# Order of VectorE's exponential tiles, forced emptying, booked durations and buffers by layer kind in a four-layer attention kernel

## The chip, the cores and the metric

The kernel runs on one core of one Trainium2 chip. The metric is the device time of one execution in microseconds. Five engines matter here: TensorE (PE in the profile, PEld its weight loads), VectorE (DVE), ScalarE (ACT), GpSimd (POOL) and SyncE (SP), which issues the DMAs. Each engine works through its own instructions in the order in which they were built; between engines, semaphores make one wait for another.

## The reference

Four layers, A, B, A, B, over one sequence of 2048 positions with 512 features. Each layer adds to x an attention over the layer-normed x, with 32 heads of 16 features:

```python
qkv = (x @ wqkv).reshape(B, S, 3, H, Dh).transpose(2, 0, 3, 1, 4)
q, k, v = qkv[0], qkv[1], qkv[2]
scores = einsum("bhqd,bhkd->bhqk", q, k) * Dh ** -0.5
# layer A only: scores = where(0 <= i - j < 256, scores, -1e9)
p = softmax(scores, axis=-1)
o = einsum("bhqk,bhkd->bhqd", p, v).transpose(0, 2, 1, 3).reshape(B, S, D) @ wo
x = x + A(layernorm(x)); x = x + B(layernorm(x)); x = x + A(layernorm(x)); x = x + B(layernorm(x))
```

A is the sliding window, 256 keys wide (layers 0 and 2, "window layers"); B looks at all 2048 keys (layers 1 and 3, "full layers").

## The kernel before

**Tiles.** Scores are made transposed, with keys on the partitions. The 32 heads are taken as eight groups of four, and the queries as four chunks of 512; one group with one chunk is called a quad, so a layer has 32 quads. A quad of a full layer goes over 16 blocks of 128 keys. For each block TensorE makes two PSUM tiles `s` of 128 x 2 x 512 (two heads each, L754), ScalarE takes their exponential into two tiles `e` (L762), and TensorE multiplies these with the values into the accumulator `acc` (L827). A quad of a window layer has three steps of two tiles (scores L758, exponential L762); GpSimd zeroes what lies outside the window (L919, L922), and TensorE multiplies with the values (L929). There are two PSUM buffers for `s` and `EB` = 5 buffers for `e`.

**The queue of value products.** `pvq` holds the value products that are not yet given to TensorE. In a window layer `flush(2)` keeps two steps in it after the scores of a new one; in a full layer `flush(1)` keeps one.

**VectorE's exponential tiles.** In a full layer, key block `DJ` = 7 of a quad can have its exponentials made on VectorE instead of ScalarE. `expect` announces a quad's unit, which may take up to two tiles `d`. `unit` lets TensorE make the scores into a separate PSUM tile `b` (L772), VectorE turn them into a fixed-point exponent (L778, 128 x 1024), and then appends six steps to VectorE's queue number 3: for each half of the tile, step a (L786, L787: integer operations), step b (L793, L794) and step c (L797, L798: a polynomial). `units` decides whether there is still time for another tile before the quad's end, by the planner's own clock. If a quad has fewer than two tiles by its last two blocks, its block 7 is made last, with ScalarE making what is missing (the "own" case in `attn_full`; the exponential then has a bias, `lead`). Otherwise the unit's value product is given as soon as it is ready, or by force with the quad's last block (`unit_values`).

**The planner.** The order of the instructions of a full layer is written out by the Python code while it builds. It keeps two clocks: `clock` for TensorE, moved by `spent`, and `vt_` for VectorE, moved by `vec`. VectorE's work waits in five queues `VQ`: 0 for splitting projected queries and keys, 1 for finishing a quad's output, 2 for the layer norm, 3 for the exponential tiles, 4 for checks of the weights (`verify`). `soon` appends a step with a booked duration. `drain()` without a number gives steps while VectorE's clock is less than `AHEAD` past TensorE's, the first queue first; queue 3 goes behind queue 4 when the foremost unit is not that of the quad in work:

```python
order = VQ[:2] + VQ[3:4] if PH["mid"] else VQ if not UX or UX[0]["quad"] == PH["quad"] else VQ[:3] + VQ[4:] + VQ[3:4]
```

`drain(4)` gives all that stands in queues 0 to 3 at once. It is called ahead of the value product of block 7, in the own case and in the forced case. After a quad's last value product, `epilogue` empties queues 0 and 1 and then copies `acc` out of PSUM to `sa` (L432, L433, inside `join`); the next quad's first value product overwrites `acc` and so waits for that copy.

**Side work.** The projections, the output product, the layer norms and the weight checks of this and the next layer are cut into `Work` pieces, which `Side` hands to TensorE between the attention's own products. `CW` is the chain of weight checks, 32 parts of one load and five VectorE instructions (L370 to L376); each part waits for the one before it.

Of the kernel before, what the change touches and what calls it, by code (L numbers as in the profile page):

```python
# [10 lines left out]
F32 = mybir.dt.float32  # L11
# [9 lines left out]
P = 128  # L21
# [14 lines left out]
EB, XB, XNB, WB, VB, OB = 5, 4, 4, 2, 3, 5  # L36
# [159 lines left out]
def fast_path(ctx, tc, flag, a_x, a_wqkv, a_wo, b_wqkv, b_wo, out):  # L196
# [11 lines left out]

    ps_x = ExitStack()
# [10 lines left out]
    OL, OFREE = [], set()  # L220
# [28 lines left out]
    def drain(upto=None):  # L249

        if upto is not None:
            if PH["mid"] and upto > 2:
                give(VQ[3])
            for q in VQ[:upto]:
                while q:
                    while q[0][2] and not q[0][2]():
                        PH["side"].one(True)
                    give(q)
            return
        while vt_[0] <= clock[0] + AHEAD:  # L260
            order = VQ[:2] + VQ[3:4] if PH["mid"] else VQ if not UX or UX[0]["quad"] == PH["quad"] else VQ[:3] + VQ[4:] + VQ[3:4]
            q = next((q for q in order if q and (q[0][2] is None or q[0][2]())), None)
            if q is None:
                return
            give(q)
# [124 lines left out]
    def phase(l):  # L390

        PH["full"], PH["win"] = l is not None and l % 2 == 1, l is not None and l % 2 == 0
# [352 lines left out]
    def exps(name, kt, qt, pr, pieces, **bias):  # L745
# [15 lines left out]
        e = pp.tile([P, 2, QC], F32, name=f"e{name}", tag="e", bufs=EB)  # L761
# [3 lines left out]
    def unit(u):  # L765
# [10 lines left out]
        t = pp.tile([P, 2, QC], I32, name=f"d{n}", tag="d", bufs=2)  # L776
        vec(1.2)
# [3 lines left out]
        for h in range(2):  # L781
# [20 lines left out]
            for us, f in ((0.92, a), (1.2, b), (1.2, c)):  # L802
                soon(3, us, f)

    def units():
# [4 lines left out]
        if u["quad"] == PH["quad"]:  # L810
            queued = sum(us for q in VQ[:4] for us, _, _ in q)
            if max(vt_[0], clock[0]) + queued + 8.5 > PH["end"]:
                return False
# [4 lines left out]
    def expect(l, c, qd, kts, qt, us):  # L818

        UX.append(dict(n=f"{l}_{c}_{qd}", quad=(l, c, qd), kt=kts[DJ // 8], qt=qt, e=[], left=0, at=0.0, shut=False, ready=clock[0] + us))  # L820
# [9 lines left out]
    def unit_values(l, c, qd, force=False):  # L830
# [4 lines left out]
        if force:  # L835
            drain(4)
# [35 lines left out]
    def attn_full(l, c, qd, kt, qt, a):  # L872
        js = [j for j in range(NT) if j != DJ]
        own = [None]
        for j in js + [DJ]:
# [17 lines left out]
            def pv(j=j, es_=es_):  # L893
                if j == js[-1] and not own[0] and UX and UX[0]["quad"] == (l, c, qd):
                    unit_values(l, c, qd, True)
                if j == DJ:
                    drain(4)
# [208 lines left out]
    def attention(l, works):  # L1106
# [5 lines left out]
        for t in range(NHT if l == 3 else 1):  # L1112
            for c in range(NQ):
# [12 lines left out]
                for qd in qds:  # L1126
# [6 lines left out]
                    a = acc[qd % 2 if win else 0]  # L1133
                    PH["side"], PH["quad"], PH["end"] = sd, (l, c, qd), clock[0] + 1.81 * NT
# [163 lines left out]
    def side1():  # L1298
        m = [(ty, s) for ty in range(2) for s in range(4)]
        a = [CW(*x, [("C", *y)] if y else [("Q", 1, 2)]) for y, x in zip([None] + m, m)]  # L1300
# [73 lines left out]
```

## Time and profile before

| | us |
|---|---|
| median of three runs | 2881.78 (2879.71 to 2884.62) |
| the profiled execution | 2883.96 |
| its span, first to last instruction | 2882.2 |
| busy TensorE, ScalarE, VectorE, GpSimd | 2526.1, 2292.2, 2021.3, 479.3 |
| stretch of layer 0 (window) | 55 to 446 |
| stretch of layer 1 (full) | 504 to 1482 |
| stretch of layer 2 (window) | 1500 to 1808 |
| stretch of layer 3 (full) | 1864 to 2848 |

The stretches reach from a layer's first exponential to its last. Between them TensorE ends the projections of the next layer. The mean granted TensorE clock was 0.975.

How to read it: a group line gives source line, engine, operation, out<-in, shapes and count, then busy us and the mean ns of one, then the idle time of the engine before them and what ended most of it. A wait line reads "engine tile line <- whom it waited for: us in total, times, longest us". A row of the timeline has the start and the length in us, engine, line and operation, how many follow each other (x), and in brackets the idle time before it. All line numbers are those of the kernel before.

### The profile page before, as it was taken

How to read it: one execution, taken by the hardware profiler on the slowest of the kernel's cores; microseconds unless marked ns; L12 is line 12 of the kernel's file. 1: busy time of each engine (PE TensorE's matmuls, PEld its weight loads, DVE VectorE, ACT ScalarE, POOL GpSimd, SP SyncE). 2: the span in 40 equal slices, each digit the busy share in tenths (PEclk: the TensorE clock that was granted, in tenths of full speed). 3: DMA queues.
4: the chain of work that ended last, by engine and by line, in shares of the span. 5: the costliest groups of instructions: out<-in, count | busy, mean ns of one | idle time of the engine just before them, and what ended most of it. 6: DMA issues, size and time to landing. Idle time of an engine off the chain costs nothing.

```text
span 2882.2 us, 112925 instructions
## 1 busy us (share of the span) xinstructions
PE 2526.1 (88%) x50177; PEld 1098.3 (38%) x50177; DVE 2021.3 (70%) x3882; ACT 2292.2 (80%) x2576; POOL 479.3 (17%) x1047
## 2 busy tenths in 40 slices
PE   7779989999998998889888887898899889888886
PEld 3233334443433443344333332543344434333332
DVE  5564454587787767768877555477788777888886
ACT  4565653999998997889865666399899989888995
POOL 1445551000000000000014667000000000000000
PEclk9999999999999999999999999999999999999998
DMA  8887866222223223222336554523223333333433
GB/s 278 227 229 232 238 177 200 65 80 80 85 91 94 86 86 97 85 76 83 114 103 195 173 149 132 161 67 102 75 89 93 99 91 102 94 98 114 123 116 112
DMA packets 335042, 359.71 MB, mean 125 GB/s; under 512 B 113616, under 2 KB 250320, under 8 KB 328144
## 3 DMA queue, kind: packets, MB, share of 16 engines
q1 hardware_dynamic: 334544, 352.40, 40.3%
q8 instruction: 394, 6.46, 0.9%
q14 instruction: 104, 0.85, 0.1%
HBM read 239.60 MB, written 96.99 MB: 117 GB/s over the span
## 4 chain that ended last, share of the span: by engine, by line
ACT 34%; PE 31%; DVE 21%; issue 8%; DMA 4%; POOL 1%; SPq 1%; ACTq 0%; DVEq 0%; POOLq 0%
ACT e L762 33%; PE b L419 9%; PE acc L827 8%; PE acc L929 4%; PE s L754 3%; PE b L416 2%; DVE d L778 2%; PE s L758 2%; PE bs L419 2%; DVE x L701 2%; DVE dp L797 2%; DVE dp L794 1%; DVE dp L793 1%; DVE d L798 1%; DVE d L787 1%
## 5 line engine op out<-in xcount | busy, mean ns | idle before, releaser
L762 ACT ACTIVATE e<-s 128x1024 f32<-128x1024 f32 (+2 forms) x2304 | 2150.2, 1043 | 315.7 <-PE s L754 150.5
L827 PE MATMUL acc<-e,vt 64*17 64x512 f32 x15496 | 1069.1, 596 | 26.8 <-DVE sa L432 26.8
L754 PE MATMUL s<-qt,kt 64*32 64x512 f16 x15496 | 827.9, 382 | 112.4 <-ACT e L762 88.8
L754 PEld LDWEIGHTS <-kt 64*32 64x32 f16 x15496 | 374.7, 90 | 837.6 <-issue 764.4
L827 PEld LDWEIGHTS acc<-e,vt 64*17 64x17 f32 x15496 | 271.8, 93 | 117.5 <-DVE sa L432 28.3
L922 POOL TENSOR_SCALAR_AFFINE_SELECT e<-e 128x256 f32<-128x256 f32 x512 | 228.9, 450 | 211.4 <-ACT e L762 209.6
L919 POOL TENSOR_SCALAR_AFFINE_SELECT e<-e 128x256 f32<-128x256 f32 x448 | 191.5, 432 | 138.7 <-ACT e L762 137.8
L758 PE MATMUL s<-qt,kt 64*128 64x384 f16 (+2 forms) x1408 | 130.8, 280 | 90.5 <-ACT e L762 72.7
L929 PE MATMUL acc<-e,vt 128*17 128x384 f32 (+2 forms) x2816 | 199.5, 395 | 4.3 <-POOL e L919 3.4
L540 POOL TENSOR_TENSOR sq_h<-sp_h 128x512 bf16<-128x512 f16 x27 | 39.7, 1471 | 912.2 <-DVE sp_h L534 892.2
L778 DVE TENSOR_SCALAR d<-b 128x1024 int32<-128x1024 f32 x111 | 135.4, 1220 | 77.9 <-PE b L772 77.9
L540 POOL TENSOR_TENSOR sq<-sp 128x512 bf16<-128x512 f16 x28 | 41.0, 1464 | 891.9 <-DVE sp L534 836.1
L419 PE MATMUL b<-xc,w 128*128 128x512 f16 x696 | 163.3, 385 | 7.4 <-DMA w<-wd 5.0
L797 DVE SCALAR_TENSOR_TENSOR dp<-dp,dm 128x512 f32<-128x512 f32 x222 | 158.4, 714 | 6.6
L794 DVE SCALAR_TENSOR_TENSOR dp<-dp,dm 128x512 f32<-128x512 f32 x222 | 154.5, 696 | 7.7
L798 DVE SCALAR_TENSOR_TENSOR d<-dp,d 128x512 f32<-128x512 f32 x222 | 153.6, 692 | 7.5
L793 DVE SCALAR_TENSOR_TENSOR dp<-dm 128x512 f32<-128x512 f32 x222 | 154.4, 695 | 0.2
L432 DVE TENSOR_SCALAR sa<-acc 128x512 f32<-128x512 f32 x64 | 44.2, 690 | 132.1 <-PE acc L827 131.9
L720 DVE STREAM_TRANSPOSE ot<-acc 128x512 f32<-128x512 f32 x64 | 45.6, 712 | 119.3 <-PE acc L929 119.1
L758 PEld LDWEIGHTS <-kt 64*128 64x128 f16 x1408 | 54.3, 95 | 195.2 <-issue 168.7
L419 PEld LDWEIGHTS <-w 128*128 128x128 f16 x816 | 76.8, 99 | 121.9 <-issue 35.5
L416 PE MATMUL b<-xc,w 64*32 64x512 f16 x2688 | 115.0, 379 | 5.3 <-DVE j L433 3.9
(151 smaller groups left out, 2606.6 us busy)
## 6 DMA issues: line engine op xcount, KB each, us to landing
kt<-kf SPq DMA_DIRECT2D x128, 512.0 KB
qt<-qs SPq DMA_DIRECT2D x128, 256.0 KB
xd<-x SPq DMA_DIRECT2D x96, 256.0 KB
x<-xd SPq DMA_DIRECT2D x96, 256.0 KB
w<-wd SPq DMA_DIRECT2D x22, 1024.0 KB
kt<-kw SPq DMA_DIRECT2D x64, 256.0 KB
qs<-sp SPq DMA_DIRECT2D x48, 256.0 KB
wo<-wd SPq DMA_DIRECT2D x12, 1024.0 KB
```

The lines of the kernel that those rows point to most:

```text
L419: nc.tensor.matmul(ps, a, b, start=(i == 0), stop=(i == len(pairs) - 1))
L754: nc.tensor.matmul(ps[g:g + 32, h], kt[R * h:R * h + R, pr, kc + g:kc + g + 32], qt[R * h:R * h + R, pr], start=True, stop=True, skip_grou ...
L758: nc.tensor.matmul(ps[:, h, s0:s0 + wd_], kt[R * h:R * h + R, pr, kc:kc + P], qt[R * h:R * h + R, pr, qc:qc + wd_], start=True, stop=True)
L762: nc.scalar.activation(e[:, :, w0:w1], ps[:, :, w0:w1], AF.Exp, scale=SCALE, **bias)
L778: nc.vector.tensor_scalar(t, ps, SCALE * LOG2E * 2.0 ** 23, -2.0 ** 30, op0=ALU.mult, op1=ALU.max)
L793: nc.vector.scalar_tensor_tensor(p[0], f, POLY[3], f, op0=ALU.add, op1=ALU.mult)
L794: nc.vector.scalar_tensor_tensor(p[0], p[0], POLY[2], f, op0=ALU.add, op1=ALU.mult)
L797: nc.vector.scalar_tensor_tensor(p[0], p[0], POLY[1], m[0].bitcast(F32), op0=ALU.add, op1=ALU.mult)
L827: nc.tensor.matmul(acc[r][32 * h:32 * h + DH + 1, :], V[l, qd // 4, j // 8][k, j % 8, 4 * (qd % 4) + h, :], es[h // 2][k, h % 2, :], start ...
L919: nc.gpsimd.affine_select(v, v, pattern=[[0, 2], [-1, P]], compare_op=ALU.is_gt, fill=0.0, base=0, channel_multiplier=1)
L922: nc.gpsimd.affine_select(v, v, pattern=[[0, 2], [1, P]], compare_op=ALU.is_ge, fill=0.0, base=0, channel_multiplier=-1)
L929: nc.tensor.matmul(a[32 * h:32 * h + DH + 1, q * P:(q + nb) * P], V[l, (4 * c + j) // 4][:, j % 4, 4 * qd + h, :], es_[h // 2][:, h % 2, s ...
```

## The change

- `EB` becomes a pair: seven buffers of `e` in window layers and five in full layers. The buffers lie in a pool of their own, closed and opened anew in `phase` when the kind of layer changes; the two buffers of `d` move into this pool.
- Units get a running number, and quads of full layers are counted in `PH["i"]`. Queue 3 keeps its place ahead of queue 4 as long as the foremost unit belongs to the quad in work or to one before it.
- `complete(u)` replaces `drain(4)` in both places: it gives steps of queue 3 until the unit that is needed has none left. The other queues, and tiles of later units, stay where they are.
- Booked durations: the fixed-point step 1.3 instead of 1.2; steps a, b, c 0.82, 1.45, 1.45 instead of 0.92, 1.2, 1.2; the time that must be left before the quad's end for a further tile 9.0 instead of 8.5.
- The chain of weight checks may start after the upper values of layer 1's first chunk (`("V", 1, 0, (1,), 0)`) instead of after the queries of its third (`("Q", 1, 2)`).

The diff:

```diff
--- before.py
+++ after.py
@@ -33,7 +33,7 @@
 LOG2E = 1.4426950408889634
 MM = 0.222
 HEAD_START = 100
-EB, XB, XNB, WB, VB, OB = 5, 4, 4, 2, 3, 5
+EB, XB, XNB, WB, VB, OB = (7, 5), 4, 4, 2, 3, 5
 RINGS = WB, VB
 L_MIN = 2.0 ** -90
 L_SUM = 2.0 ** 60
@@ -206,6 +206,8 @@
     ps_c = pool("ps_c", 1, space=bass.MemoryType.PSUM)
     ps_s = pool("ps_s", 2, space=bass.MemoryType.PSUM)
 
+    pe_x = ExitStack()
+    ctx.push(pe_x)
     ps_x = ExitStack()
     ctx.push(ps_x)
     dp = pool("scr", 1, space=bass.MemoryType.DRAM)
@@ -217,7 +219,7 @@
     XC, XN, V, O, OT, KM, PH = {}, {}, {}, {}, {}, {}, {"free": 0.0, "busy": False, "mid": False}
     WT, ST, pend = {}, {}, []
     VQ, vt_, UX = [deque() for _ in range(5)], [0.0], deque()
-    OL, OFREE = [], set()
+    OL, OFREE, QN = [], set(), [0]
 
     clock, DONE, XNR, ONR = [0.0], {}, {}, {}
 
@@ -258,7 +260,7 @@
                     give(q)
             return
         while vt_[0] <= clock[0] + AHEAD:
-            order = VQ[:2] + VQ[3:4] if PH["mid"] else VQ if not UX or UX[0]["quad"] == PH["quad"] else VQ[:3] + VQ[4:] + VQ[3:4]
+            order = VQ[:2] + VQ[3:4] if PH["mid"] else VQ if not UX or UX[0]["i"] <= PH["i"] else VQ[:3] + VQ[4:] + VQ[3:4]
             q = next((q for q in order if q and (q[0][2] is None or q[0][2]())), None)
             if q is None:
                 return
@@ -389,6 +391,10 @@
 
     def phase(l):
 
+        if l is not None and PH.get("es") != l % 2:
+            PH["es"] = l % 2
+            pe_x.close()
+            PH["ep"] = pe_x.enter_context(tc.tile_pool(name=f"exps{l}", bufs=EB[l % 2]))
         PH["full"], PH["win"] = l is not None and l % 2 == 1, l is not None and l % 2 == 0
         if PH["full"] or not PH["win"] and "pool" not in PH or l is None and PH.get("halves"):
             ps_x.close()
@@ -758,7 +764,7 @@
                 nc.tensor.matmul(ps[:, h, s0:s0 + wd_], kt[R * h:R * h + R, pr, kc:kc + P],
                                  qt[R * h:R * h + R, pr, qc:qc + wd_], start=True, stop=True)
         spent(0.23 if PH["full"] else 0.27)
-        e = pp.tile([P, 2, QC], F32, name=f"e{name}", tag="e", bufs=EB)
+        e = PH["ep"].tile([P, 2, QC], F32, name=f"e{name}", tag="e")
         nc.scalar.activation(e[:, :, w0:w1], ps[:, :, w0:w1], AF.Exp, scale=SCALE, **bias)
         return e
 
@@ -773,8 +779,8 @@
                                  u["qt"][R * h:R * h + R, pr], start=True, stop=True, skip_group_check=True)
         spent(0.27)
         PH["free"] = clock[0] + 1.5
-        t = pp.tile([P, 2, QC], I32, name=f"d{n}", tag="d", bufs=2)
-        vec(1.2)
+        t = PH["ep"].tile([P, 2, QC], I32, name=f"d{n}", tag="d", bufs=2)
+        vec(1.3)
         nc.vector.tensor_scalar(t, ps, SCALE * LOG2E * 2.0 ** 23, -2.0 ** 30, op0=ALU.mult, op1=ALU.max)
         u["e"].append(t.bitcast(F32))
         u["left"] += 2
@@ -799,7 +805,7 @@
                 u["left"] -= 1
                 PH["mid"] = False
                 u["at"] = vt_[0] + 0.4
-            for us, f in ((0.92, a), (1.2, b), (1.2, c)):
+            for us, f in ((0.82, a), (1.45, b), (1.45, c)):
                 soon(3, us, f)
 
     def units():
@@ -809,7 +815,7 @@
             return False
         if u["quad"] == PH["quad"]:
             queued = sum(us for q in VQ[:4] for us, _, _ in q)
-            if max(vt_[0], clock[0]) + queued + 8.5 > PH["end"]:
+            if max(vt_[0], clock[0]) + queued + 9.0 > PH["end"]:
                 return False
         if not PH["busy"] and clock[0] >= PH["free"]:
             unit(u)
@@ -817,7 +823,13 @@
 
     def expect(l, c, qd, kts, qt, us):
 
-        UX.append(dict(n=f"{l}_{c}_{qd}", quad=(l, c, qd), kt=kts[DJ // 8], qt=qt, e=[], left=0, at=0.0, shut=False, ready=clock[0] + us))
+        QN[0] += 1
+        UX.append(dict(n=f"{l}_{c}_{qd}", quad=(l, c, qd), kt=kts[DJ // 8], qt=qt, e=[], left=0, at=0.0, i=QN[0], shut=False, ready=clock[0] + us))
+
+    def complete(u):
+
+        while u["left"]:
+            give(VQ[3])
 
     def values_of(l, qd, j, es, first, last):
 
@@ -833,7 +845,7 @@
         if u["quad"] != (l, c, qd) or u["shut"]:
             return False
         if force:
-            drain(4)
+            complete(u)
         elif len(u["e"]) < 2 or u["left"] or clock[0] < u["at"]:
             return False
         UX.popleft()
@@ -894,7 +906,7 @@
                 if j == js[-1] and not own[0] and UX and UX[0]["quad"] == (l, c, qd):
                     unit_values(l, c, qd, True)
                 if j == DJ:
-                    drain(4)
+                    complete(own[0])
                 values_of(l, qd, j, es_, j == 0, j == (DJ if own[0] else js[-1]))
             yield pv
 
@@ -1131,6 +1143,7 @@
                     if nxt and not win:
                         expect(l, c, qd + 1, *nxt, 6.0)
                     a = acc[qd % 2 if win else 0]
+                    PH["i"] = PH.get("i", 0) + (not win)
                     PH["side"], PH["quad"], PH["end"] = sd, (l, c, qd), clock[0] + 1.81 * NT
                     began, u = clock[0], 0
                     for f in (attn_win if win else attn_full)(l, c, qd, *ops, a):
@@ -1297,7 +1310,7 @@
 
     def side1():
         m = [(ty, s) for ty in range(2) for s in range(4)]
-        a = [CW(*x, [("C", *y)] if y else [("Q", 1, 2)]) for y, x in zip([None] + m, m)]
+        a = [CW(*x, [("C", *y)] if y else [("V", 1, 0, (1,), 0)]) for y, x in zip([None] + m, m)]
         a += [Q(1, c, False) for c in (2, 3)]
         for c in range(3):
             a += [OO(1, c), T(2, c)] + ([Q(2, c - 1, False)] if c else []) + [K(2, c, False)] + ([VV(2, c, False)] if c < 2 else [])
```

## Prediction

> **What bounds the kernel now.** I read the head of the page first, then the busy time by stage, then the waits of each kind of stage, then two short timelines.
>
> ```profile
> span 2882.2 us, 112925 instructions
> PE 2526.1 (88%) x50177; PEld 1098.3 (38%) x50177; DVE 2021.3 (70%) x3882; ACT 2292.2 (80%) x2576; POOL 479.3 (17%) x1047
> 55.00:446.00 391.00, 339.71 (x2952) 135.38 (x2951) 203.66 (x476) 237.96 (x308) 196.19 (x486) 0.94 0.78 222
> 504.00:1482.00 978.00, 886.13 (x21944) 390.50 (x21936) 741.63 (x1363) 903.74 (x973) 37.32 (x28) 0.98 0.28 86
> 1500.00:1808.00 308.00, 253.03 (x2553) 100.39 (x2552) 184.13 (x459) 195.65 (x228) 195.75 (x479) 1.00 0.53 157
> 1864.00:2848.00 984.00, 877.82 (x21438) 384.12 (x21438) 784.00 (x1339) 900.31 (x966) 39.72 (x27) 0.99 0.31 97
> ```
>
> The last four rows are layers 0 (window), 1 (full), 2 (window) and 3 (full): length, then busy PE, PEld, DVE, ACT, POOL, granted clock, DMA share, GB/s. In a full layer ScalarE sets the pace: 903.7 us of 978, about 0.931 us for each of its 971 exponential tiles. What is lost there is 74 and 84 us of idle ScalarE. In a window layer TensorE is nearest to full, and lacks 51 us (391.0 - 339.7) in layer 0 and 55 us (308.0 - 253.0) in layer 2.
>
> The waits of layer 0, of layer 2 (between them a line of dots), then of layers 1 and 3:
>
> ```profile
> PE s L758 <- ACT e L762: 24.9, 32, 1.6
> ACT e L762 <- PE acc L929: 21.7, 36, 5.1
> ...
> PE s L758 <- ACT e L762: 47.8, 59, 1.0
> ACT e L762 <- PE acc L929: 24.8, 49, 1.0
> ACT e L762 <- POOL e L919: 13.9, 22, 0.6
> ...
> ACT e L762 <- PE s L754: 70.4, 42, 15.8
> ...
> ACT e L762 <- PE s L754: 80.2, 59, 7.1
> ```
>
> So in the window layers scores wait for ScalarE, and ScalarE for buffers; in the full layers ScalarE waits for scores, in few and long pieces.
>
> **The change, part by part.**
>
> *Seven buffers of e in the window layers.* A stretch of layer 2 without side work:
>
> ```profile
> 1791.01 0.39 PE L758 MATMUL s<-qt,kt 64*128 64x128 f16 x4
> 1791.19 1.94 ACT L762 ACTIVATE e<-s 128x1024 f32<-128x1024 f32 x2 [0.64 <-PE acc L929]
> 1792.01 1.39 POOL L922 TENSOR_SCALAR_AFFINE_SELECT e<-e 128x256 f32<-128x256 f32 x2
> 1792.27 0.40 PE L758 MATMUL s<-qt,kt 64*128 64x128 f16 x4 [0.87 <-ACT e L762]
> 1792.59 1.06 PE L929 MATMUL acc<-e,vt 128*17 128x256 f32 x16
> 1793.36 0.40 POOL L919 TENSOR_SCALAR_AFFINE_SELECT e<-e 128x256 f32<-128x256 f32 x1
> 1793.58 0.39 PE L758 MATMUL s<-qt,kt 64*128 64x256 f16 x4
> 1784.00:1804.00 20.00, 13.39 (x190) 5.27 (x191) 17.95 (x41) 14.99 (x16) 19.06 (x43) 1.00 0.74 183
> ```
>
> One step (two tiles) takes 1793.58 - 1791.01 = 2.57 us. The queue of value products is two steps deep: four tiles are held while two are made, six in all. With five buffers the sixth exponential starts only when a value product has ended (0.64 us idle), and the next scores need its PSUM bank (0.87 us idle on PE). With seven no tile waits so. Then a step is paced by the slowest of three: PE's own 2.57 - 0.87 = 1.70 us; ScalarE's two tiles at 1.94 - 1.02 = 0.92 us each, about 1.9 us with the handing over; or GpSimd, whose 960 selects over 192 steps are five a step. In the last row, columns as before, 43 selects take 19.06 us of 20: 2.2 us a step. So of each wait 0.20 us stays if ScalarE paces, 0.50 us if GpSimd does. I take 0.45, since GpSimd is 95% busy in the row just where the waits are. Layer 2: 47.8 - 59 x 0.45 = 21.3 us; layer 0: 24.9 - 32 x 0.45 = 10.5 us. Together **-32 us**. Bounds: none, if selects go on at 1.39 us for two (3.5 us a step, more than 2.57 already); all 72.7 us at best. The order of PE's instructions in layers 0 and 2 is the same in both kernels, so no other cost hides there. A new e pool is opened at each change of kind; its first tile comes behind value products that PE has already passed, so I cost it at nothing (at worst one wait of 0.6 us per layer).
>
> The Trainium skill, "SBUF — State Buffer", section "Who interferes with whom", says that a VectorE instruction with two SBUF inputs holds, for its whole length, a port that GpSimd needs. The trace agrees in kind: two selects took 1.39 us where one alone took 0.40. By that rule alone, buffers could not help while VectorE normalizes, and this term would be near 0.
>
> *Emptying stops at the tile needed.* Layer 1, from the quad with one VectorE tile to the next:
>
> ```profile
> 881.91 0.61 PE L827 MATMUL acc<-d,vt 64*17 64x512 f32 x4
> 882.14 0.43 DVE L786 TENSOR_SCALAR dm<-d 128x512 int32<-128x512 int32 x1
> ...
> 888.69 0.69 DVE L798 SCALAR_TENSOR_TENSOR d<-dp,d 128x512 f32<-128x512 f32 x1
> 889.30 0.68 DVE L432 TENSOR_SCALAR sa<-acc 128x512 f32<-128x512 f32 x1
> 890.04 2.73 PE L827 MATMUL acc<-e,vt 64*17 64x512 f32 x16 [5.25 <-DVE sa L432]
> ...
> 893.29 1.02 ACT L762 ACTIVATE e<-s 128x1024 f32<-128x1024 f32 x1 [7.13 <-PE s L754]
> ```
>
> The quad's own tile was done at 881.9. Yet `drain(4)` put the whole chain of the next quad's tile on VectorE, 882.14 to 889.38, ahead of the copy of `acc`, and the next quad's first product into `acc` waited 5.25 us; ScalarE lost 7.13. Over the run:
>
> ```profile
> PE acc L827 <- DVE sa L432: 26.8, 5, 6.2
> PE acc L827 <- DVE d L798: 20.7, 14, 4.9
> ```
>
> Five such places, 26.8 us of PE, times 7.13 / 5.25 = 36.4 us of ScalarE. In the new stream of VectorE four of them have nothing heavy left ahead of the copy; the fifth, late in layer 1, still has a normalization ahead of the quad's own last two halves. I leave it half of a mean stall, 3.6 us: **-33 us**. What is late next: the deferred chain itself, due one quad later with some 20 us to spare.
>
> *Rank to the quad's end.* One stall is of another kind:
>
> ```profile
> 1139.38 0.69 DVE L432 TENSOR_SCALAR sa<-acc 128x512 f32<-128x512 f32 x1 [3.68 <-PE acc L827]
> 1139.82 1.94 ACT L762 ACTIVATE e<-s 128x1024 f32<-128x1024 f32 x2 [15.83 <-PE s L754]
> ```
>
> There all but the first half of two tiles stood on VectorE behind a normalization and a weight check, and PE waited for them. In the new stream that quad takes one VectorE tile, finished before the copy. **-16 us**.
>
> *Durations.* One VectorE tile, from its rows:
>
> ```profile
> L778 DVE TENSOR_SCALAR d<-b 128x1024 int32<-128x1024 f32 x111 | 135.4, 1220 | 77.9 <-PE b L772 77.9
> L786 DVE TENSOR_SCALAR dm<-d 128x512 int32<-128x512 int32 x222 | 98.3, 443 | 1.3
> L787 DVE TENSOR_SCALAR d<-d 128x512 int32<-128x512 int32 x222 | 94.9, 427 | 7.6
> L793 DVE SCALAR_TENSOR_TENSOR dp<-dm 128x512 f32<-128x512 f32 x222 | 154.4, 695 | 0.2
> L794 DVE SCALAR_TENSOR_TENSOR dp<-dp,dm 128x512 f32<-128x512 f32 x222 | 154.5, 696 | 7.7
> L797 DVE SCALAR_TENSOR_TENSOR dp<-dp,dm 128x512 f32<-128x512 f32 x222 | 158.4, 714 | 6.6
> L798 DVE SCALAR_TENSOR_TENSOR d<-dp,d 128x512 f32<-128x512 f32 x222 | 153.6, 692 | 7.5
> ```
>
> 1.22 + 2 x 3.667 = 8.55 us; the planner booked 1.2 + 2 x 3.32 = 7.84, and books 1.3 + 2 x 3.72 = 8.74 now. It plans 106 tiles, not 111. Five go to ScalarE: 5 x 0.931 = **+4.7 us**; VectorE's 43 us less count only through lateness. Four quads late in layer 3 drop to one tile, some in layer 1 gain one; a late last half costs about 20.7 / 14 x 1.36 = 2.0 us of ScalarE each. I cost the exchange at **0**, with 20.7 x 1.36 = 28 us as bound to either side.
>
> *Weight checks earlier.* Thirty-two checks run either way; two more of them fall into layer 1. Their loads go past others on SP's queue, with DMA at 0.28 there. **0**; at most a late end of one chain, 2 us.
>
> **Sum.** -32 - 33 - 16 + 5 = -76 us. The profiled execution took 2883.96 us, 2.2 above the median of three: 2884 - 76 = 2808, or 2806 against the median.
>
> **Rivals.** A difference of 0.2%, 6 us, is about what can be told from no change.
>
> *GpSimd paces the window layers*, so their 32 us shrink to about 5: 2833. For it: 95% busy in the row above. Against: over all of layer 2 it is 195.8 of 308, so side work lets it catch up.
>
> *The stalls move.* The deferred chains pile up at the next quad's end, and of the 44 us net in the full layers 10 stay: 2840. For it: VectorE is at 742 of 978. Against: quads that inherit a chain also make one tile less.
>
> *More is gained.* ScalarE paces the window steps (54.5 us instead of 32) and half of the late-half waits go (14): 2769. For it: tiles booked at their true length come less late. Against: GpSimd's row again.
>
> *Slower.* The longer bookings place the last half of a tile about 2 x 0.4 + 0.1 = 0.9 us later in the stream, where it may fall behind a VectorE instruction that waits for PE, and the product at the quad's end waits for both. If that costs 2.0 us in each of the 42 quads with two VectorE tiles, it is 84 us and eats the gain; from 2.3 us each the kernel ends at 2900. Against: idle time before L793 is 0.2 us in 222, so the chain is seldom held up by what stands before it.
>
> *Nothing happens*, if the planner's gains in one layer are lost in another: 2880.
>
> **How the numbers follow.** My case 0.42 (2785 to 2825), GpSimd 0.17, stalls move 0.15, more 0.18, slower 0.06, nothing 0.02. The predicted time is my case's, 2806. The range 2758 to 2848 takes in the two smaller gains and the larger one with its bounds. Faster 0.92, same 0.02, slower 0.06.
>
> **What would show it.** Right: no PE wait for `sa` near 26.8 us (I expect under 6), no idle ScalarE of 7 us at a quad's start, the wait of L758 for e under 45 us in all, layer 2 near 287 us, layer 1 near 935, the tile d 106 times. Wrong: POOL at 90% in layer 2 with PE waiting for its selects at L929 (new name of the line: 941), or waits of L827 for the last half well over 20.7 us.

## The result, and the profile after

The changed kernel takes 2835.96 us, median of four runs (2831.43 to 2838.99), against 2880.74 for the kernel before in the same sitting (2878.34 to 2884.62): a ratio of 0.9842, 95% interval 0.9822 to 0.9862. The gain is 45 us, where 76 had been forecast.

Line numbers move: the scores of full layers are now L760 (before L754), those of window layers L764 (L758), the exponential L768 (L762), the last step of a VectorE half L804 (L798), value products L839 and L941 (L827, L929), the copy to `sa` L438 (L432). In the experiments they differ by a few lines more; the operation and the tile name them.

The first line of the page after, and, from the list of instruction groups, the lines for the exponential and for the value products of window layers:

```profile
span 2837.2 us, 112864 instructions
...
L768 ACT ACTIVATE e<-s 128x1024 f32<-128x1024 f32 (+2 forms) x2304 | 2138.4, 1044 | 257.8 <-PE s L760 139.5 <-PE s L764 103.9 <-POOL e L931 6.2
...
L941 PE MATMUL acc<-e,vt 128*17 128x384 f32 (+2 forms) x2816 | 205.8, 398 | 5.2 <-POOL e L931 4.0 <-DVE ot L726 0.8 <-POOL e L934 0.2
```

The busy time by stage after, layers 0 to 3 (columns as in the prediction):

```profile
56.00:437.00 381.00, 340.83 (x2943) 135.58 (x2944) 201.03 (x476) 233.08 (x308) 194.37 (x484) 0.94 0.79 228
495.60:1448.70 953.10, 879.98 (x22016) 390.96 (x22023) 739.52 (x1364) 903.35 (x973) 38.73 (x29) 0.99 0.29 89
1461.00:1750.60 289.60, 257.55 (x2546) 100.95 (x2546) 187.02 (x445) 190.43 (x228) 189.70 (x473) 0.98 0.56 166
1808.40:2809.40 1001.00, 885.42 (x21494) 387.96 (x21486) 758.00 (x1291) 904.75 (x970) 39.72 (x27) 0.99 0.31 97
```

TensorE's waits after: two rows of the whole run, then, below the dots, two of layer 3 alone, and last the row of layer 3 before that answers to the fourth:

```profile
PE acc L839 <- DVE d L804: 37.3, 19, 3.3
PE s L764 <- ACT e L768: 35.7, 59, 1.6
...
ACT e L768 <- PE s L760: 93.0, 52, 6.9
PE acc L839 <- DVE d L804: 25.9, 13, 3.2
```

```profile
PE acc L827 <- DVE d L798: 11.2, 7, 2.5
```

The wait for `sa` has no row any more, and layer 2 lasts 289.6 us: the two large steps happened. But layer 3 is longer than before, 1001.0 against 984.4, though no copy of `acc` is late in it; in its place TensorE waits for last halves of VectorE tiles, 25.9 us against 11.2, and ScalarE for scores 93.0 against 80.2. Layer by layer, from first to last exponential, the change was -10.1, -24.3, -18.6 and +16.6 us; the stretches outside the layers gave 8.6 more. The pause between layers 1 and 2 became 5.6 us shorter and the stretch behind layer 3, from its last exponential to the end, 6.6 us (34.4 to 27.8); the others became some 3.5 us longer. Most of that is work that moved: the pause has 81 matmuls fewer, the stretch behind layer 3 has 48 fewer, and layers 1 and 3 make them instead.

### The profile page after: what moved, and what is told of

It reads as the page before. It is cut to its first block, busy times and chain, and to the rows that moved or that the text cites. A ratio compares the mean times of both kernels' runs of the same rounds, so it can differ in the third digit from the quotient of the medians.

```text
span 2837.2 us, 112864 instructions
## 1 busy us (share of the span) xinstructions
PE 2528.1 (89%) x50177; PEld 1102.0 (39%) x50177; DVE 1991.0 (70%) x3817; ACT 2285.2 (81%) x2581; POOL 474.6 (17%) x1047
## 4 chain that ended last, share of the span: by engine, by line
ACT 36%; PE 33%; DVE 16%; issue 9%; DMA 3%; POOL 2%; SPq 1%; ACTq 0%; DVEq 0%; POOLq 0%
ACT e L768 36%; PE b L425 9%; PE acc L839 9%; PE s L760 4%; PE b L422 3%; PE acc L941 3%; PE bs L425 2%; PE s L764 2%; DVE dp L803 1%; DVE dp L799 1%; DVE d L784 1%; DVE x L707 1%; DVE d L804 1%; DVE dp L800 1%; POOL e L931 1%
## 5 line engine op out<-in xcount | busy, mean ns | idle before, releaser
L768 ACT ACTIVATE e<-s 128x1024 f32<-128x1024 f32 (+2 forms) x2304 | 2138.4, 1044 | 257.8 <-PE s L760 139.5
L839 PE MATMUL acc<-e,vt 64*17 64x512 f32 x15536 | 1069.4, 593 | 0.2 <-issue 0.2
L760 PE MATMUL s<-qt,kt 64*32 64x512 f16 x15536 | 827.6, 382 | 114.7 <-ACT e L768 90.0
L760 PEld LDWEIGHTS <-kt 64*32 64x32 f16 x15536 | 376.8, 90 | 835.7 <-issue 759.4
L839 PEld LDWEIGHTS acc<-e,vt 64*17 64x17 f32 x15536 | 271.2, 93 | 86.7 <-issue 28.4
L941 PE MATMUL acc<-e,vt 128*17 128x384 f32 (+2 forms) x2816 | 205.8, 398 | 5.2 <-POOL e L931 4.0
L784 DVE TENSOR_SCALAR d<-b 128x1024 int32<-128x1024 f32 x106 | 129.3, 1220 | 79.0 <-PE b L778 78.8
L764 PE MATMUL s<-qt,kt 64*128 64x384 f16 (+2 forms) x1408 | 128.5, 280 | 56.0 <-ACT e L768 35.7
L803 DVE SCALAR_TENSOR_TENSOR dp<-dp,dm 128x512 f32<-128x512 f32 x212 | 152.3, 718 | 6.2
L800 DVE SCALAR_TENSOR_TENSOR dp<-dp,dm 128x512 f32<-128x512 f32 x212 | 146.7, 692 | 7.4
L804 DVE SCALAR_TENSOR_TENSOR d<-dp,d 128x512 f32<-128x512 f32 x212 | 146.7, 692 | 7.2
L438 DVE TENSOR_SCALAR sa<-acc 128x512 f32<-128x512 f32 x64 | 44.2, 691 | 144.8 <-PE acc L839 144.3
L839 PE MATMUL acc<-d,vt 64*17 64x512 f32 x848 | 100.0, 606 | 38.3 <-DVE d L804 37.3
L425 PEld LDWEIGHTS <-w 128*128 128x128 f16 x816 | 77.4, 100 | 123.0 <-issue 37.5
L422 PE MATMUL b<-wo,oh 64*32 64x512 f16 x2592 | 111.3, 384 | 7.5 <-DVE x L707 4.6
```

What stands on the lines that cost most here:

```text
L422: nc.tensor.matmul(ps[g:g + 32, r], a[k, g:g + 32], b[k], start=(i == 0), stop=(i == len(pairs) - 1), skip_group_check=True)
L425: nc.tensor.matmul(ps, a, b, start=(i == 0), stop=(i == len(pairs) - 1))
L760: nc.tensor.matmul(ps[g:g + 32, h], kt[R * h:R * h + R, pr, kc + g:kc + g + 32], qt[R * h:R * h + R, pr], start=True, stop=True, skip_grou ...
L764: nc.tensor.matmul(ps[:, h, s0:s0 + wd_], kt[R * h:R * h + R, pr, kc:kc + P], qt[R * h:R * h + R, pr, qc:qc + wd_], start=True, stop=True)
L768: nc.scalar.activation(e[:, :, w0:w1], ps[:, :, w0:w1], AF.Exp, scale=SCALE, **bias)
L800: nc.vector.scalar_tensor_tensor(p[0], p[0], POLY[2], f, op0=ALU.add, op1=ALU.mult)
```

## The experiments

Twelve kernels, each run beside the kernel before on the same chip. Layers are from first to last exponential; "pause" is the time from the last exponential of layer 1 to the first of layer 2; "late" is TensorE's wait for last halves of VectorE tiles in layers 1 and 3. The VectorE tiles of layers 1 and 3 stand in the last column. All but the ratio comes from one profiled execution. A difference of a few us in one layer means little: layer 0 alone took 379.4 to 383.8 us in the kernels with seven buffers.

| kernel | ratio, 95% interval | layer 0 | 1 | 2 | 3 | pause | late | tiles |
|---|---|---|---|---|---|---|---|---|
| before | 1 | 391.2 | 977.4 | 308.2 | 984.4 | 17.9 | 9.3 / 11.2 | 53 / 58 |
| after | 0.984 [0.982, 0.986] | 381.1 | 953.1 | 289.6 | 1001.0 | 12.3 | 11.3 / 25.9 | 52 / 54 |
| e1_old_bookings | 0.978 [0.976, 0.980] | 379.4 | 948.8 | 290.8 | 976.8 | 19.3 | 7.8 / 11.9 | 53 / 58 |
| e2_buffers_only | 0.992 [0.991, 0.994] | 382.7 | 978.7 | 288.4 | 984.0 | 18.2 | 9.0 / 11.9 | 53 / 58 |
| e3_complete_only | 0.999 [0.998, 1.000] | 388.9 | 973.9 | 301.4 | 973.0 | 34.0 | 22.2 / 11.9 | 50 / 58 |
| e4_bookings_only | 1.008 [1.006, 1.011] | 392.2 | 979.2 | 308.7 | 1025.9 | 11.9 | 13.9 / 25.3 | 48 / 54 |
| e5_checks_held | 0.976 [0.974, 0.978] | 383.7 | 949.0 | 280.9 | 975.1 | 19.2 | 7.7 / 11.8 | 53 / 58 |
| e6_complete_checks_held | 0.993 [0.991, 0.994] | 392.5 | 973.3 | 303.0 | 975.6 | 10.7 | 22.1 / 13.8 | 50 / 58 |
| e7_old_rank | 0.982 [0.980, 0.984] | 383.8 | 970.3 | 281.2 | 977.1 | 12.7 | 22.1 / 11.7 | 50 / 58 |
| e8_before_norm | 0.972 [0.970, 0.974] | 383.7 | 937.7 | 280.1 | 972.7 | 22.8 | 1.3 / 11.8 | 53 / 58 |
| e9_new_steps_more_tiles | 1.001 [1.000, 1.002] | 380.7 | 971.9 | 288.5 | 1024.5 | 19.6 | 24.2 / 38.4 | 56 / 57 |
| e10_old_steps_fewer_tiles | 0.979 [0.978, 0.981] | 382.5 | 953.7 | 280.2 | 959.1 | 36.4 | 11.0 / 2.0 | 51 / 54 |
| e11_short_steps | 0.994 [0.992, 0.996] | 382.5 | 975.2 | 279.4 | 1008.1 | 16.2 | 4.9 / 9.7 | 54 / 62 |
| e12_norm_fewer_tiles | 0.963 [0.960, 0.965] | 382.0 | 936.7 | 282.1 | 956.9 | 15.6 | 0.2 / 2.0 | 50 / 54 |

**The change with the old booked durations.**

```diff
-        vec(1.3)
+        vec(1.2)
...
-            for us, f in ((0.82, a), (1.45, b), (1.45, c)):
+            for us, f in ((0.92, a), (1.2, b), (1.2, c)):
...
-            if max(vt_[0], clock[0]) + queued + 9.0 > PH["end"]:
+            if max(vt_[0], clock[0]) + queued + 8.5 > PH["end"]:
```

> The changed kernel with the old bookings (1.2; 0.92, 1.2, 1.2; 8.5) put back, all else as changed. Layer 3 took 984 us before and 1001 us after. Theory A, the new bookings place the last half of a tile later in VectorE's stream and that costs layer 3: layer 3 falls to about 977 us (984 less the one own-case stall of 7), the wait of the value products for d falls from 37 us to about 21, total about 2815 us. Rival B, the smaller emptying leaves work that piles up at later quads' ends: layer 3 stays near 1000 us, total 2836 us.

Layer 3 came back from 1001.0 to 976.8 us, and the kernel took 2821.01. Layer 3 of this kernel, the stage and two waits:

```profile
1810.70:2787.50 976.80, 875.26 (x21446) 385.38 (x21446) 783.83 (x1339) 899.77 (x966) 39.73 (x27) 0.99 0.32 98
...
ACT e L768 <- PE s L760: 74.1, 55, 6.9
...
PE acc L839 <- DVE d L804: 11.9, 7, 2.8
```

The new bookings cost some 24 us in layer 3. Of these 5.5 come back behind it: the stretch behind layer 3 lasts 33.3 us here and 27.8 in the changed kernel, which makes 48 of the last output products inside the layer. How the rest arises, one quad shows. In layer 3 of the changed kernel (a stretch of the timeline, VectorE and the end of the quad):

```profile
2604.93 1.42 DVE L707 SCALAR_TENSOR_TENSOR x<-b,x 128x512 f32<-128x512 f32 x2 [2.25 <-PE b L422]
...
2608.96 1.42 DVE L707 SCALAR_TENSOR_TENSOR x<-b,x 128x512 f32<-128x512 f32 x2 [0.80 <-PE b L422]
...
2618.16 1.42 DVE L707 SCALAR_TENSOR_TENSOR x<-b,x 128x512 f32<-128x512 f32 x2 [0.64 <-PE b L422]
...
2622.27 1.41 DVE L707 SCALAR_TENSOR_TENSOR x<-b,x 128x512 f32<-128x512 f32 x2
...
2626.56 0.69 DVE L804 SCALAR_TENSOR_TENSOR d<-dp,d 128x512 f32<-128x512 f32 x1
...
2627.31 1.04 PE L839 MATMUL acc<-d,vt 64*17 64x512 f32 x2 [3.25 <-DVE d L804]
...
2631.02 3.77 ACT L768 ACTIVATE e<-s 128x1024 f32<-128x1024 f32 x4 [6.66 <-PE s L760]
```

And the same quad with the old bookings:

```profile
2592.24 1.42 DVE L707 SCALAR_TENSOR_TENSOR x<-b,x 128x512 f32<-128x512 f32 x2 [0.30 <-PE b L422]
...
2596.36 1.41 DVE L707 SCALAR_TENSOR_TENSOR x<-b,x 128x512 f32<-128x512 f32 x2
...
2605.63 1.41 DVE L707 SCALAR_TENSOR_TENSOR x<-b,x 128x512 f32<-128x512 f32 x2
...
2609.13 0.69 DVE L804 SCALAR_TENSOR_TENSOR d<-dp,d 128x512 f32<-128x512 f32 x1
...
2612.43 3.77 ACT L768 ACTIVATE e<-s 128x1024 f32<-128x1024 f32 x4 [0.91 <-PE s L760]
```

Each L707 row is a pair of additions of output products to x, which must first wait for those products on TensorE. With longer bookings VectorE's planned clock runs ahead sooner, the chain of halves is written later into its stream, and four such pairs instead of three, with 3.4 us more of waiting for TensorE (2.25 + 0.80 + 0.64 - 0.30), stand ahead of the last half's end (L804). TensorE loses 3.25 us at the quad's end, ScalarE 6.66 instead of 0.91.

**The buffers alone**, in the kernel before.

```diff
-EB, XB, XNB, WB, VB, OB = 5, 4, 4, 2, 3, 5
+EB, XB, XNB, WB, VB, OB = (7, 5), 4, 4, 2, 3, 5
...
+            PH["ep"] = pe_x.enter_context(tc.tile_pool(name=f"exps{l}", bufs=EB[l % 2]))
...
-        e = pp.tile([P, 2, QC], F32, name=f"e{name}", tag="e", bufs=EB)
+        e = PH["ep"].tile([P, 2, QC], F32, name=f"e{name}", tag="e")
```

> The kernel before with seven buffers of e in window layers and nothing else. Both theories: layer 0 near 381 us, layer 2 near 290 us, layers 1 and 3 unchanged at 977 and 984 us, total 2852 us. If the buffers owe their gain to something else in the change, layers 0 and 2 stay at 391 and 308 us and the total at 2881 us.

2859.89 us against 2885.76 of the kernel before in the same sitting, ratio 0.992: layers 0 and 2 gave 8.5 and 19.8 us, the full layers stayed. The buffers' term stands: 25.9 us in all, where the expectation had 29 (2881 to 2852). In layer 2 of this kernel:

```profile
PE s L764 <- ACT e L768: 20.4, 36, 1.0
```

It was 47.8 us in 59 waits. No GpSimd wait replaced it: POOL is busy 191 of the layer's 288 us.

**`complete` alone**, in the kernel before.

```diff
         if force:
-            drain(4)
+            complete(u)
...
                 if j == DJ:
-                    drain(4)
+                    complete(own[0])
```

> The kernel before with the smaller emptying (complete) and nothing else. Theory A: the wait for sa (26.8 us) goes, layer 3 falls to about 977 us and layer 1 by some 25 to 45 us, total 2835 to 2850 us. Rival B: layer 3 rises to 995 us or more, total near 2860 us.

Layer 3 gained 11.4 us, where 7 had been expected for its one stall, and the wait for `sa` is gone in both layers. Yet the kernel stayed at 2880.26, ratio 0.999. Two things took the gain. In layer 1 the chains that are no longer emptied by force came late one quad later: TensorE waited 22.2 us for last halves, 12.9 more than before. Layer 1 gained 3.5 us in all. And the pause before layer 2 grew from 17.9 to 34.0, although about a hundred of its matmuls had moved into layer 1. The timeline of that pause (a load, the parts of the weight checks, then the projection's copy `j` and the products that need it):

```profile
1473.33 1.10 DVE L370 TENSOR_REDUCE wa<-wc 128x128 f32<-128x512 f32 x1 [2.55 <-DMA wc<-in_B_wqkv_dram]
...
1487.25 1.02 DVE L370 TENSOR_REDUCE wa<-wc 128x128 f32<-128x512 f32 x1 [2.61 <-DMA wc<-in_B_wo_dram]
...
1489.84 0.69 DVE L433 SCALAR_TENSOR_TENSOR j<-b,j 128x512 f32<-128x512 f32 x1
1490.59 2.76 PE L416 MATMUL b<-xc,w 64*32 64x512 f16 x48 [16.02 <-DVE j L433]
```

Four checks stand one behind the other on VectorE's stream, each waiting some 2.6 us for a load that the one before it released, and the copy behind them kept TensorE idle for 16 us. They had been given in layer 2, whose order on VectorE is not written out by hand, and moved forward to the end of layer 1. Layer 2, which had ten checks before and has none here, became 6.8 us shorter in turn.

**The bookings alone**, in the kernel before (the three edits of the first experiment the other way round).

> The kernel before with the new bookings alone. Theory A: layer 3 rises from 984 us to about 1005 us and the wait for d from 20.7 us to over 30, total 2890 to 2910 us. Rival B: layer 3 stays at 984 us or falls, total 2881 us or less.

2908.14 us, ratio 1.008: +22 us. Layer 3 is 41.5 us longer, though 15.5 of these come back in the stretch behind it (34.4 to 18.9 us), where 152 of 182 matmuls have moved into the layer. The longer bookings are a loss by themselves, and they bring stalls at the copy to `sa` back into layer 3 as well (15.7 us, from 5.2).

**Weight checks held**: the first experiment, with the checks that are left after layer 1 kept back until layer 3.

```diff
+            while not PH["full"] and not PH.get("over"):
+                yield wait(5)
...
+    PH["over"] = True
```

> As the run with the old bookings (2821 us), but weight checks that remain after layer 1 wait for layer 3 instead of running in layer 2. Theory C, the checks off the quads' ends cost nothing: total 2815 to 2825 us, the pause between layers 1 and 2 stays near 18 us, layer 3 rises by at most 4 us from 977. Rival: eight checks more in layer 3 cost their 16 us of VectorE, total 2835 us. It is the base for the two runs below.

2815.35 us; ratio 0.976. Here the pause did not shrink (19.2; it was 19.3), layer 2 became 9.9 us shorter instead. So the checks cost time in a window layer too. The other kernels with seven buffers agree: layer 2 took 279.4 to 282.1 us with at most one check in it, and 288.4 to 290.8 with eight to ten.

**`complete` alone, with the checks held**: the third experiment and the edit above.

> The kernel before with the smaller emptying, and the checks held as above. The smaller emptying alone gave only 5 us, with layer 3 at 973 us as forecast, but 34 us instead of 18 between layers 1 and 2, where checks that each waited for their load stood ahead of a projection's copy. Theory D, that was the whole loss at the boundary: the pause falls back to 18 us or so and the total to about 2865 us. Rival: the pause has another cause and stays above 30 us, total 2880 us. In both, layer 1 stays near 974 us, because the wait for d in it (22 us) has another cause.

The pause fell from 34.0 to 10.7 us and the kernel to 2863.07, ratio 0.993. Layer 1 stayed at 973.3, so the checks explain the pause and not layer 1.

**The old rank**, in the kernel with the checks held.

```diff
-            order = VQ[:2] + VQ[3:4] if PH["mid"] else VQ if not UX or UX[0]["i"] <= PH["i"] else VQ[:3] + VQ[4:] + VQ[3:4]
+            order = VQ[:2] + VQ[3:4] if PH["mid"] else VQ if not UX or UX[0]["quad"] == PH["quad"] else VQ[:3] + VQ[4:] + VQ[3:4]
```

> As e5 with the old rank rule (queue 3 behind queue 4 unless the foremost unit is that of the quad in work). Theory E, rank is what made the smaller emptying pay in layer 1: layer 1 rises from 949 to about 970 us, with the wait for d there back over 18 us, total 2840 us. Rival, rank is worth nothing: layer 1 at 949 us, total as e5.

The kernel took 2832.53 us. Layer 1 went from 949.0 to 970.3 us and late halves from 7.7 to 22.1. TensorE's wait for them in layer 1, with the new rank and with the old one:

```profile
PE acc L841 <- DVE d L806: 7.7, 5, 3.0
```

```profile
PE acc L841 <- DVE d L806: 22.1, 10, 4.9
```

The rank is worth 21 us in layer 1 and 17 in the kernel, since with the old rank the pause is 6.5 us shorter (12.7; 19.2) and layer 1 makes about a hundred of its matmuls. But it is not worth this where it had been sought: the stall of 15.83 us that the prediction quotes is still 15.3 us long with the old rank and 14.0 with the new one.

**Queue 3 ahead of the layer norm**, in the kernel with the checks held.

```diff
-            order = VQ[:2] + VQ[3:4] if PH["mid"] else VQ if not UX or UX[0]["i"] <= PH["i"] else VQ[:3] + VQ[4:] + VQ[3:4]
+            order = VQ[:2] + VQ[3:4] if PH["mid"] else VQ[:2] + VQ[3:4] + VQ[2:3] + VQ[4:] if not UX or UX[0]["i"] <= PH["i"] else VQ[:3] + VQ[4:] + VQ[3:4]
```

> As e5 with queue 3 also ahead of queue 2 (the layer norm) as long as the foremost unit belongs to the quad in work or an earlier one. Theory F, the 14 us stall that is left in layer 1 (quad 2,5) comes from the normalization that is given ahead of the chain of an unfinished tile: the stall goes, layer 1 falls from 949 to about 933 us, total 14 to 18 us under e5, near 2805 us. Rival, the norm that is now later holds up the side work: layer 1 stays, or the pause after it grows, total as e5 or more.

2804.22 us, ratio 0.972; layer 1 went from 949.0 to 937.7, and the pause grew by 3.6 us. The timeline of that stall with the checks held shows its cause (the end of a norm, the late halves, the next exponential):

```profile
1103.27 0.55 DVE L469 TENSOR_SCALAR xn<-x,mv,y 128x512 f32<-128x512 f32 x1
...
1109.24 0.69 DVE L475 TENSOR_TENSOR xh<-xn,xh 128x512 f16<-128x512 f32 x1
...
1109.85 0.42 DVE L794 TENSOR_SCALAR dm<-d 128x512 int32<-128x512 int32 x1
...
1113.56 1.04 PE L841 MATMUL acc<-d,vt 64*17 64x512 f32 x4 [3.03 <-DVE d L806]
...
1124.84 1.94 ACT L770 ACTIVATE e<-s 128x1024 f32<-128x1024 f32 x2 [13.99 <-PE s L762]
```

And with queue 3 ahead of the norm:

```profile
1103.36 0.69 DVE L806 SCALAR_TENSOR_TENSOR d<-dp,d 128x512 f32<-128x512 f32 x1
...
1106.34 0.55 DVE L469 TENSOR_SCALAR xn<-x,mv,y 128x512 f32<-128x512 f32 x1
...
1110.63 1.94 ACT L770 ACTIVATE e<-s 128x1024 f32<-128x1024 f32 x2 [0.83 <-PE s L762]
```

The norm lies in queue 2, which no rank in queues 3 and 4 touches. With the halves written first, the norm runs behind them and 13.99 us of idle ScalarE become 0.83.

**New steps, more tiles**: the changed kernel with 7.0 instead of 9.0 us to be left for a further tile.

```diff
-            if max(vt_[0], clock[0]) + queued + 9.0 > PH["end"]:
+            if max(vt_[0], clock[0]) + queued + 7.0 > PH["end"]:
```

> The changed kernel with its new step bookings, but the time that must be left before the quad's end cut from 9.0 to 7.0, so that layer 3 makes 57 tiles on VectorE instead of 54. The longer bookings cost layer 3 some 24 us (1001 against 977). Theory G, by where the steps are placed: layer 3 stays at 1000 us or rises. Rival H, by the tiles that go back to ScalarE: layer 3 falls to about 983 us.

**Old steps, fewer tiles**: the first experiment with 10.0 instead of 8.5.

```diff
-            if max(vt_[0], clock[0]) + queued + 8.5 > PH["end"]:
+            if max(vt_[0], clock[0]) + queued + 10.0 > PH["end"]:
```

> The changed kernel with the old bookings and 10.0 instead of 8.5 before the quad's end, so that layer 3 makes 54 tiles on VectorE, as the changed kernel does. Theory G, placement: layer 3 stays at 974 to 982 us. Rival H, number of tiles: layer 3 rises to about 1000 us.

These two take apart what the bookings did in layer 3: where the halves are placed, and how many tiles there are. The kernels took 2885.74 and 2823.34 us. Layer 3 with new steps and 57 tiles, then with old steps and 54:

```profile
PE acc L839 <- DVE d L804: 38.4, 22, 3.4
```

```profile
1824.80:2783.90 959.10, 865.59 (x21446) 384.76 (x21438) 752.73 (x1287) 904.86 (x970) 39.73 (x27) 0.99 0.33 99
...
ACT e L768 <- PE s L760: 50.9, 49, 4.8
...
PE acc L839 <- DVE d L804: 2.0, 1, 2.0
```

| layer 3 | 57 or 58 tiles | 54 tiles |
|---|---|---|
| old steps | 976.8 (late 11.9) | 959.1 (late 2.0) |
| new steps | 1024.5 (late 38.4) | 1001.0 (late 25.9) |

At 54 tiles the placement costs 41.9 us, of which 23.9 of late wait, times 7.13 / 5.25 as in the prediction, are 32. Fewer tiles gain 18 to 24 us in either row. The new steps also shorten the stretch behind layer 3 (27.5 and 27.8 us, against 33.3 and 35.5 with the old ones), because 48 output products stand inside the layer; counted with it, the placement costs 34 us at 54 tiles and 42 at 57 or 58, and fewer tiles gain 16 to 23. The two kernels with 54 tiles do not have them in the same quads, so place and number are not fully parted here: much of what fewer tiles gain is again late halves, 9.9 us in the upper row, or some 13 of ScalarE by the same factor.

Both expectations for the second kernel had layer 3 at 974 us or above, and it took 959.1. That four more tiles on ScalarE should make the layer longer was wrong in sign: with the old steps ScalarE works 5.1 us more (904.86 - 899.77) and is idle for want of scores 23.2 us less (74.1 - 50.9). The gain of the second kernel did not reach the total: five checks had moved to the end of layer 1 again, with a pause of 36.4 us.

**Still shorter steps**: the kernel of the eighth experiment with shorter bookings than the old ones.

```diff
-            for us, f in ((0.92, a), (1.2, b), (1.2, c)):
+            for us, f in ((0.8, a), (1.0, b), (1.0, c)):
...
-            if max(vt_[0], clock[0]) + queued + 8.5 > PH["end"]:
+            if max(vt_[0], clock[0]) + queued + 9.0 > PH["end"]:
```

> The fastest so far (2804 us) with steps booked shorter still (0.8, 1.0, 1.0) and 9.0 before the quad's end; 62 tiles on VectorE in layer 3 instead of 58. Theory G, the earlier a chain stands in the stream the better: layer 3 falls from 973 to 960 us or less, total 2785 to 2795 us. Rival, VectorE is full by then, and the chains end late whatever their place: layer 3 at 975 us or more, total 2805 us or more.

2866.49 us, ratio 0.994: layers 1 and 3 became 37.5 and 35.4 us longer, and the theory's figures failed. The rival had the size, but not its reason: late halves are few (9.7 us in layer 3), but there are 62 tiles, and other waits of TensorE grew. Layer 3 of this kernel:

```profile
ACT e L770 <- PE s L762: 100.8, 71, 11.4
...
PE b L424 <- DVE km L589: 10.8, 4, 4.9
PE acc L841 <- DVE d L806: 9.7, 13, 1.5
...
PE acc L841 <- DVE sa L440: 4.8, 6, 1.9
```

Projections now wait for VectorE behind the chains (`km` 10.8 us against 4.8), and the copy to `sa` is late again. These rows add up to less than the 35.4 us by which layer 3 grew. How much of it is the tiles' number and how much their place was not taken apart: shorter steps with no more tiles were not run.

**Together**: the eighth experiment with 10.0 instead of 8.5.

```diff
-            if max(vt_[0], clock[0]) + queued + 8.5 > PH["end"]:
+            if max(vt_[0], clock[0]) + queued + 10.0 > PH["end"]:
```

> The kernel that keeps the exponential tiles ahead of the layer norm, with the old step durations, the checks left after layer 1 held back, and 10.0 instead of 8.5 us to be left before the quad's end for a further tile: 50 tiles in layer 1 and 54 in layer 3 (before this edit 53 and 58). Theory I: the gains found so far are of different places and add up. Layer 3 near 957 us (972.7 before this edit; the same edit took 976.8 to 959.1 where the norm stood ahead), layer 1 within 5 of 938 (three tiles more on ScalarE are 2.8 us), the pause between layers 1 and 2 at most 24 us, because the checks that took 36.4 us of pause in the run with fewer tiles cannot be hoisted to the end of layer 1: total 2785 to 2795. Rival J: what was gained in layer 3 by fewer tiles came from the layer norm's place and not from the tiles; with the norm behind the tiles layer 3 stays at 968 or above, the total at 2802 or above. Rival K: fewer tiles leave layer 1 short of VectorE's help, as ScalarE paces it: layer 1 at 948 or above and the total no better than 2800, whatever layer 3 does.

2777.54 us (2773.5 to 2782.91); ratio 0.963, interval 0.960 to 0.965, better than both kernels of the comparison. Layers 1 and 3, and ScalarE's wait for scores in layer 1, then in layer 3:

```profile
495.80:1432.50 936.70, 869.22 (x21949) 388.32 (x21955) 729.44 (x1366) 908.11 (x975) 37.00 (x28) 1.00 0.30 92
...
ACT e L770 <- PE s L762: 23.1, 34, 3.9
...
1787.20:2744.10 956.90, 862.38 (x21446) 381.92 (x21446) 754.66 (x1296) 904.60 (x970) 39.72 (x27) 1.00 0.32 100
...
ACT e L770 <- PE s L762: 48.7, 50, 4.2
```

The gains add up, and both rivals fall: layer 3 reached 956.9 with the norm behind the tiles, and layer 1 did not miss the three tiles. The total is 7.5 us below the forecast of 2785 to 2795, of which the pause explains 7 (15.6 us; 22.8 before this edit).

## Why the prediction was right, and where it was wrong

The direction, and the range of 2758 to 2848, held; the point, 2806, was 30 us too low, and the time lies outside the 2785 to 2825 that the prediction called its own case. That the range held was in part luck: it had been made wide enough for two rivals, "GpSimd paces" (2833) and "the stalls move" (2840). The first did not happen. Of the second the size came true, since the full layers gained 7.7 us net (24.3 - 16.6) where 10 were to stay, but its cause is not enough: with the old bookings the same emptying and rank keep 36 us there (28.6 + 7.6).

Of the signs that the prediction named, the waits for `sa` and for L758 and the 106 tiles came as said, and layer 2 nearly (289.6; 287). Layer 1 did not (953; 935), and one idle stretch of ScalarE over 7 us was left. A sign of being wrong did come: the waits for last halves rose to 37.3 us, well over 20.7.

*Buffers, -32.* Right: layers 0 and 2 gave 10.1 and 18.6 us where 10.5 and 21.3 stood, and alone they gave 8.5 and 19.8. The wait of scores for ScalarE fell from 72.7 to 35.7 us (91 waits at 0.45 would have left 41). GpSimd does not pace: over layer 2 it is busy 189.7 us of 289.6, and TensorE waits 4.2 us for selects in the whole run. By the Trainium skill's rule on the shared port that the prediction weighed ("SBUF — State Buffer", "Who interferes with whom") this term would have been near 0; the mean select is 0.44 us here, between the 0.40 of one alone and the 0.70 of two in 1.39 beside VectorE's work, so selects are slowed in places, but the gain is not lost.

*Emptying, -33.* The waits for the copy went at all five places, as forecast. What came next was mis-sized. The deferred chain was given "some 20 us to spare"; `complete` alone shows it late in layer 1 (12.9 us more wait, some 17 of ScalarE). In the change itself the new rank repairs that. The fifth place, for which 3.6 us were left, the quad late in layer 1 with a norm ahead of its halves, kept its whole stall. The exponential behind it, in the kernel before and then after:

```profile
1398.88 13.91 ACT L762 ACTIVATE e<-s 128x1024 f32<-128x1024 f32 x15 [8.11 <-PE s L754]
```

```profile
1364.42 8.36 ACT L768 ACTIVATE e<-s 128x1024 f32<-128x1024 f32 x9 [10.53 <-PE s L760]
```

ScalarE is idle for 10.53 us there, after 8.11 before and 1.89 at an earlier exponential of that quad. TensorE waits there for the quad's own last halves now (3.35 and 1.97 us), and no longer for the copy (6.22 us). With the old bookings, emptying and rank together gave layer 1 28.6 us (977.4 to 948.8), where some 41 stood for the two terms.

*Rank, -16.* The size was about right by luck, and the place wrong. The rank is worth 21 us in layer 1 by making the deferred chains early, a thing that the prediction had booked at nothing; the 15.83 us stall at 1139.8 belongs to the norm in queue 2. In the changed kernel that quad has one tile, as forecast, and the stall is still a third of what it was:

```profile
1119.92 1.02 ACT L768 ACTIVATE e<-s 128x1024 f32<-128x1024 f32 x1 [4.93 <-PE s L760]
```

What was gained there comes with the new bookings and not with the rank: they leave the quad one tile, where the old ones give it two, and with these the stall stays 14.0 us long.

*Durations, +5 and an exchange at 0.* This is the step that failed. In layer 3, where -3 us were forecast, +16.6 came. The bookings cost 24 us there beside the other parts and 41.5 alone, with the placement alone at 42 (34 when the stretch behind the layer is counted with it) and fewer tiles paying some 18 back. The bound of 28 us "to either side" was too narrow for the placement, since it took only the late waits that existed already. The tiles that go to ScalarE, at 0.931 us each, were right as work and wrong as a price: four fewer tiles made layer 3 shorter. The rival "slower" named the mechanism, the last half behind a VectorE instruction that waits for TensorE, and got 0.06; the idle time before L793, used against it, is small because the waiting instruction itself carries the idle time, and the chain follows without a gap.

*Weight checks, 0.* The earlier start was not run alone. In the changed kernel layer 1 has two checks more, as forecast, and the pause fell to 12.3 us; but which of them land at the end of layer 1 decides up to 23 us (34.0 to 10.7 us), so a 0 with 2 us as worst case was too bold.

By layer the miss of 31 us is: layer 1 17 us (24.3 gained; 41 forecast, with four of the five stalls, the rank and one of the five tiles there), layer 3 20, layers 0 and 2 3, less 9 from the stretches outside, from which matmuls moved into layers 1 and 3. In layer 1 two places carry 12 of the 17: 7 us at the fifth stall (10.5 - 3.6) and 5 left at the quad of the rank's term. The other 5 were not traced to a place.

## What to carry to other kernels

A booked duration in a planner is a place in a queue, not a measurement: setting it to the traced length moved work behind instructions that wait for others here, so change placement and amount apart and look at each stage by itself, together with the stretch behind it, into which or out of which work may move. Look for what stands ahead of late work in an in-order engine's stream, and give that work its rank against every queue, not only against the one next to it. Fewer items on a helper engine can make the bottleneck faster, even though the bottleneck then does more itself.

## What the runs showed of the hardware

The pause before layer 2 shows what an idle TensorE costs beyond the wait. The same 140 or so matmuls, with `complete` alone and then with the checks held (stage rows, columns as before):

```profile
1475.20:1509.20 34.00, 10.30 (x140) 3.37 (x139) 16.56 (x42) 0.00 (x0) 3.72 (x5) 0.60 0.36 117
```

```profile
1479.10:1489.80 10.70, 5.71 (x141) 2.45 (x141) 6.99 (x14) 0.08 (x2) 3.73 (x5) 1.00 0.65 189
```

Their busy time is 10.30 us at a granted clock of 0.60, and 5.71 at 1.00. On a smaller scale 16 value products took 2.73 us behind the 5.25 us stall that the prediction quotes, and 1.05 us elsewhere: some 0.8 us of that is a wait for the second step of the copy (L433), and the granted clock was 0.50 from 890 to 893 us. That TensorE is throttled after standing still and comes back only with sustained work is what the Trainium skill says ("TensorE: Matmul & The Clock Gate", Part 1); these rows agree. So a stall's price to ScalarE (7.13 us for 5.25) includes the rest of the copy and the slow products behind it.
